# A mixture-of-experts layer on one core: left-over slots of experts 1 to 7 move to the first block, with 32-column float32 matmuls on four column groups for their output

## The chip, the core and the metric

The kernel runs on one core of a Trainium2 chip. A core has five engines that run their own queues of instructions: TensorE (PE; its weight loads are listed apart as PEld), VectorE (DVE), ScalarE (ACT), GpSimd (POOL) and SyncE (SP), which only issues transfers here. They meet through semaphores. The metric is the device time of one execution in microseconds; the time of a kernel is the median of its runs.

## The reference

Local attention (8 heads, chunks of 64) gives 4608 tokens of 512 numbers. A noisy gate picks two of eight experts for each token, and the output is the weighted sum of the two experts' results. This is the part that the change touches:

```python
N, D, E, F = (4608, 512, 8, 1024)
for e in range(E):
    for k in range(2):
        mask = top2[:, k] == e
        h = np.maximum(x[mask] @ w1[e], 0.0)
        out[mask] += top2_w[mask, k, None] * (h @ w2[e])
```

All is in float32, and the result must agree with it to float32 accuracy.

## The kernel before

**Stages.** First attention and the gate, with lists built on the way: for each expert a list of token rows in slots of 128 (`lid`, `lfl`) and of weights (`lwt`). Expert 0 takes its slots first; experts 1 to 7 are ordered by their count on the chip. How many slots a place has is fixed ahead of time (`CAPS`, L30): 1216, 1216, 1184, 1184, 1184, 1152, 1152, 1152. That is nine full tiles of 128 slots for each, and for the first five a left-over tile of 64, 64, 32, 32 and 32. The order of work is written out by hand in the code; each engine runs its instructions in the order of the code.

**Blocks.** `blocks_of` (L37) makes three blocks of each expert: tiles 0 to 2, 3 to 5 and 6 to 9. The left-over tile is the fourth of the third block. Blocks are numbered `i` from 0 to 23, three to an expert. The loop at L698 emits layer 1 of block `i` and then layer 2 of block `i - 1` (blocks 0 to 2 differ a little).

**Layer 1** (`layer1`, L286) computes h transposed: for each of 8 slices `f` of the hidden dimension, 4 x 3 matmuls with a 128x128 piece of W1 as weights and the block's slots as moving columns. Float32 is split into a high and a low part (`xh`, `xl`, `w1h`, `w1l`), and `three` (L277) issues three products of parts in float32r, which are all on L284. ScalarE's Relu writes `hh`, VectorE writes the rest `hl`.

**Layer 2** (`layer2`, L307) turns the roles round: for each tile of up to 128 slots, and each of 8 slices, three matmuls with `hh` or `hl` of the tile as weights and 512 columns of `w2h` or `w2l` moving. A left-over tile of 32 or 64 slots takes the same 24 matmuls of 512 columns as a full one. `weigh` (L301) multiplies by the slots' weights, and `store` (L249) adds the rows to the output in memory by an indirect transfer on POOL.

**Weights.** `w_load` (L109, SP's queue) brings W1 and W2 in four pieces each through four `st` buffers; `w_split` (L119) makes the high and low parts on ScalarE and VectorE. The loads of W1 for expert e + 1 are issued at the block with b = 1 (L700), into the buffers that W2 of expert e leaves when it is split in the same block's layer 1. The split of W1 for e + 1 stands in layer 2 of that block, after layer 1 of the third one.

**Tokens.** From block 3 on, a tile's token rows are fetched in quarters of 32 slots (`gather_some`, L227): an indirect transfer on POOL brings, for 32 slots, 4 pieces of 128 numbers each to 128 partitions, by the indices in `piece`. VectorE turns them in 32x32 squares (`x_tile`, L258). `pieces` (L197) makes these indices in layer 2 of block 1, by four matmuls that spread 32 slots over four groups of partitions; and after it the tiles of block 3 are fetched at once (`gathered(3, 3)`, L734).

Of the kernel before, what the change touches and what calls it, by code (L numbers as in the profile page):

```python
# [8 lines left out]
FT = mybir.dt.float32  # L9
FR = mybir.dt.float32r  # L10
# [3 lines left out]
AF = mybir.ActivationFunctionType  # L14
OP = mybir.AluOpType
# [4 lines left out]
P = 128  # L20
NTOK = 4608
NT = NTOK // P
DM = 512
NE = 8
FF = 1024
ND = DM // P
NF = FF // P
# [9 lines left out]
def blocks_of(cap):  # L37

    rows = [min(P, cap - s) for s in range(0, cap, P)]
    out, cur = [], []  # L40
    for j, r in enumerate(rows):
        cur.append((j, r))
        if len(cur) == 3 and len(rows) - j - 1 != 1:
            out.append(cur)
            cur = []
    if cur:
        out.append(cur)
    return out


@with_exitstack
def kernel(ctx, tc, qT, kT, vh, wgn, noise, w1, w2, out, caps=CAPS):
    nc = tc.nc
    consts = ctx.enter_context(tc.tile_pool(name="consts", bufs=1))
# [35 lines left out]
    for c in sorted(set(caps[1:])):  # L90
        n = caps.index(c, 1)
# [13 lines left out]
    staged = {}  # L105
# [23 lines left out]
    PS = ctx.enter_context(tc.tile_pool(name="psum", bufs=1, space=PSUM)).tile([P, 8, 512], FT, name="PS")  # L129
# [2 lines left out]

    blocks = [blocks_of(c) for c in caps]
    nb = len(blocks[0])
    assert all(len(b) == nb for b in blocks)
    BL = [(e, b) for e in range(NE) for b in range(nb)]
# [1 line left out]
    NJ = NLIST  # L140
    BN = max(sum(r for _, r in b) for bs in blocks for b in bs)
# [15 lines left out]
    lwt = consts.tile([P, NJ, NE], FT, name="lwt")  # L157
    lfl = consts.tile([P, NJ, NE], FT, name="lfl")
    lid0 = {b: consts.tile([P, len(blocks[0][b])], I32, name=f"lid0{b}") for b in EARLY}
    lwt0 = {b: consts.tile([P, len(blocks[0][b])], FT, name=f"lwt0{b}") for b in EARLY}  # L160
    piece = consts.tile([P, 4, NJ, NE], I32, name="piece")
    part = consts.tile([P, 1], FT, name="part")
    nc.vector.memset(part, 0.0)
    for q in range(1, 4):
        nc.vector.memset(part[q * 32:q * 32 + 32], float(q))
    xpieces = xbuf.rearrange("r (q c) -> (r q) c", c=P)
    XG, XH, HT, BX, BH, OB = {}, {}, {}, {}, {}, {}
    rot = {"xg": 0, "tr": 0, "l1": 0, "l2": 0}
    BANKS = {"tr": (0, 1), "l1": (2, 3, 4), "l2": (5, 6)}
# [2 lines left out]
    def bank(what, among=None):  # L172
        among = among or (BANKS if rot["l2"] < 6 else WIDE)[what]
        rot[what] += 1
        return PS[:, among[rot[what] % len(among)], :]

    def rows_of(i, j):
        e = BL[i][0]
        k = j - blocks[0][i][0][0] if i in EARLY else 0
        return lid0[i][:, k:k + 1] if i in EARLY else lid[:, j, e:e + 1]  # L180
# [16 lines left out]
    def pieces():  # L197

        spread = xv[0].tile([P, 4, 4, 32], FT, name="xv")
        nc.vector.tensor_copy(spread, ident.rearrange("p (t c) -> p t c", t=4)[:, :, None, :].to_broadcast([P, 4, 4, 32]))  # L200
        tf = lfl
        for t in range(4):
            p = PS[:, 7, t * NJ * NE:(t + 1) * NJ * NE]
            nc.tensor.matmul(p, spread[:, t].rearrange("p a c -> p (a c)"), tf.rearrange("p j e -> p (j e)"),
                             start=True, stop=True)
        nc.vector.tensor_scalar(piece.rearrange("p t j e -> p (t j e)"), PS[:, 7, 0:4 * NJ * NE],
                                4.0, part, op0=OP.mult, op1=OP.add)

# [37 lines left out]

    stores = {}

    def store(i, e, j, r, o):  # L249
        nc.gpsimd.memset(spacer, 0.0)  # L250
        s = nc.gpsimd.indirect_dma_start(  # L251
            out=out, out_offset=bass.IndirectOffsetOnAxis(ap=rows_of(i, j)[0:r], axis=0),
            in_=o[0:r], in_offset=None, compute_op=OP.add)
        for o in stores.setdefault(e, []):
            tc.declare_no_dep(s.ins, o.ins, reason="an expert has a token once; rows below 128 get zeros and are not read")
        stores[e].append(s)
# [29 lines left out]
    def layer1(i, hook, hook_d=lambda f, d: None):  # L286
        e, b = BL[i]
        n = sum(r for _, r in blocks[e][b])
        HT[i] = BH[i % 2]
        for f in range(NF):  # L290
            p = bank("l1", (0, 1) if i == 0 else None)[:, 0:n]
            for d in range(ND):
                three(p, W[e, 1, d], (slice(None), slice(f * P, (f + 1) * P)),
                      XH[i], (slice(None), d, slice(0, n)), d == 0, d == ND - 1)
                hook_d(f, d)
            hh, hl = HT[i][f]
            nc.scalar.activation(hh[:, 0:n], p, AF.Relu)  # L297
            nc.vector.scalar_tensor_tensor(hl[:, 0:n], p, 0.0, hh[:, 0:n].bitcast(FT), op0=OP.max, op1=OP.subtract)  # L298
            hook(f)

    def weigh(i, j, r, p):  # L301
        e = BL[i][0]
        o = OB[0].tile([P, DM], FT, name="o")
        nc.vector.tensor_scalar(o[0:r], p[0:r], weights_of(i, j)[0:r], None, op0=OP.mult)  # L304
        store(i, e, j, r, o)

    def layer2(i, hook):  # L307
        e, b = BL[i]
        tiles = blocks[e][b]
        for k, (j, r) in enumerate(tiles):  # L310
            p = bank("l2")
            for f in range(NF):
                three(p[0:r], W[e, 2, f // 2], (slice(None), slice((f % 2) * DM, (f % 2) * DM + DM)),
                      HT[i][f], (slice(None), slice(k * P, k * P + r)), f == 0, f == NF - 1, flip=True)
                hook(k, f)
            weigh(i, j, r, p)
            if i > 1:
                gather_some(2)
# [354 lines left out]
    pb = ExitStack()  # L673

    def block_bufs(q):
        pool = pb.enter_context(tc.tile_pool(name=f"blk{q}", bufs=1))
        BX[q] = tuple(pool.tile([P, ND, BN], FR, name=f"x{c}{q}") for c in "hl")
        BH[q] = [tuple(pool.tile([P, BN], FR, name=f"h{c}{q}{f}") for c in "hl") for f in range(NF)]

    block_bufs(0)  # L680
    attend(NT)
# [16 lines left out]
    for i in range(NBL + 1):  # L698
        e, b = BL[i] if i < NBL else (NE, 0)
        if b == 1 % nb and e + 1 < NE and i > 1:  # L700
            for c in range(4):
                w_load(e + 1, 1, c)
        split2 = halves if i < NBL and (b == 1 % nb if e else b == 0) else []
        nxt = blocks[BL[i + 1][0]][BL[i + 1][1]] if i + 1 < NBL else []

        def turn_next(k):
            gathered(i + 1, k)
            x_tile(i + 1, k)
            ahead[0] -= 1

        def hook1(f):
            if i > 1 and b != 1 and f % 2 == 1 and f // 2 < len(nxt):
                turn_next(f // 2)
            if split2:
                w_split(e, 2, *split2[f])
            if i > 1:
                gather_some(1 + f % 2, HT[i][f][0])

        def hook2_f(k, f):
            if i > 1 and b == 1 and f % 4 == 1 and 2 * k + f // 4 < len(nxt):  # L720
                turn_next(2 * k + f // 4)
            if (k, f) == (0, 3):
                for q in split1:
                    w_split(split1_e, 1, *q)

        def hook2_r(k, f):
            hook2_f(k, f)
            step_route(2)
            if k + 1 < len(nxt) or i == 0:
                if f == 6 and k < len(nxt):  # L730
                    x_tile(i + 1, k)
            if i == 1 and (k, f) == (0, 0):
                pieces()
                gathered(3, 3)  # L734

        if 1 < i < NBL and i == 3:
            layer2(i - 1, hook2_f)
        if i < NBL:
            layer1(i, hook1, hook_tail if i == 0 else lambda f, d: None)
        split1 = halves if (i < NBL and b == nb - 1 and e + 1 < NE) else []  # L740
        split1_e = e + 1

        if i == 0:
            pa.close()
            block_bufs(1)
            OB[0] = pb.enter_context(tc.tile_pool(name="ob", bufs=4))
        if i == 0:
            zero_out(NT)
            layer2(0, hook2_r)
            finish_route()  # L750
            for r in range(1, NE):
                place[r] = nc.values_load(order[0:1, r:r + 1], engines=[mybir.EngineType.SP], min_val=0, max_val=NE - 1)
            for c in range(4):
                w_load(1, 1, c)
            pg.close()
            later_xg.append(pb.enter_context(tc.tile_pool(name="xg2", bufs=3)))
            xy = pb.enter_context(tc.tile_pool(name="xy", bufs=2))
            xv.append(pb.enter_context(tc.tile_pool(name="xv", bufs=1)))
        elif i == 1:
            layer2(1, hook2_r)  # L760
            x_tile(2, 3)
        elif i != 2 and i != 3:
            layer2(i - 1, hook2_f)
        if split1:
            for c in range(4):
                w_load(e + 1, 2, c)
# [132 lines left out]
```

## Time and profile before

| what | value |
|---|---|
| median of 3 runs | 1031.76 us (1029.02 to 1033.64) |
| profiled execution | 1033.37 us, its span 1031.5 us |
| mean granted TensorE clock | 0.981 |
| matmuls of L284, layer 1 (3 products) | 3 x 768, mean 340 to 342 ns |
| matmuls of L284, layer 2 (3 products) | 3 x 616, mean 390 to 391 ns |
| gathers on POOL (L239) | 257, mean 1022 ns |
| stores on POOL (L251) | 77, mean 1587 ns |

A profile's span runs from the first to the last instruction; the execution's own time is somewhat longer. Records of matmuls overlap, because TensorE starts one before the last one has drained: a mean of 390 ns is the length of a record, and the distance between starts is what a matmul takes of the path. A shape such as `128*32 128x512` is rows times columns of the weights, then partitions times elements that move.

### The profile page before, as it was taken

What the parts mean: (1) busy time and instruction counts of PE and PEld (TensorE: products, weight loads), DVE (VectorE), ACT (ScalarE), POOL (GpSimd) and SP (SyncE); (2) the same over time, 40 slices, a digit from 0 to 9 for tenths busy, and PEclk for the clock granted to TensorE, in tenths of its full rate; (3) what the DMA queues carried; (4) which work ended last, traced back from release to release, by engine and by line L of the source; (5) the groups of instructions that cost most, each with busy time, mean ns of one, the idle gap of its engine ahead of it and who ended that gap; (6) DMA issues with size and microseconds to landing.
All of it is one profiled execution on the core that took longest, in us unless ns stands there. A gap on an engine that the chain in (4) does not pass through costs nothing.

```text
span 1031.5 us, 17805 instructions
## 1 busy us (share of the span) xinstructions
PE 978.0 (95%) x7121; PEld 866.5 (84%) x7121; DVE 462.0 (45%) x1030; ACT 298.3 (29%) x617; POOL 479.6 (46%) x612
## 2 busy tenths in 40 slices
PE   6778978989999999999999999999999999999995
PEld 5666757887889889888988998899889998999884
DVE  5686665562525443344334432453245334533311
ACT  3565554331314221222222321232123222322100
POOL 1142422445675666157714772378428724801111
PEclk9989888999999999999999999999999999999998
DMA  9987891142442452345224423443334334412213
GB/s 370 402 326 256 280 388 51 41 113 67 95 105 82 95 133 57 58 101 138 54 53 104 130 60 49 103 136 61 51 111 122 77 54 106 135 19 31 31 21 42
DMA packets 51445, 121.48 MB, mean 118 GB/s; under 512 B 8272, under 2 KB 8528, under 8 KB 51360
## 3 DMA queue, kind: packets, MB, share of 16 engines
q0 software_dynamic: 19664, 38.69, 21.7%
q1 hardware_dynamic: 26512, 72.20, 19.3%
q10 hardware_dynamic: 5184, 9.44, 2.4%
q8 instruction: 56, 0.92, 0.4%
q14 instruction: 29, 0.24, 0.1%
HBM read 81.56 MB, written 38.73 MB: 117 GB/s over the span
## 4 chain that ended last, share of the span: by engine, by line
PE 89%; DVE 5%; DMA 2%; ACT 1%; issue 1%; POOL 0%; SPq 0%; ACTq 0%; DVEq 0%; POOLq 0%
PE PS L284 80%; PE PS L397 2%; PE PS L549 2%; PE PS L370 2%; DMA out<-zero 1%; PE PS L386 1%; PE PS L417 1%; DVE xs L409 1%; DVE mx L374 1%; DVE pr L379 1%; PE PS L435 1%; DMA xbuf<-xs 1%; PE PS L424 1%; DMA kb<-in_kT 0%; PE PS L267 0%
## 5 line engine op out<-in xcount | busy, mean ns | idle before, releaser
L239 POOL DMA_INDIRECT xg<-xbuf,piece x257 | 262.7, 1022 | 75.9 <-issue 70.4
L251 POOL DMA_INDIRECT out<-o,lid x77 | 122.2, 1587 | 316.7 <-DVE o L304 301.4
L284 PE MATMUL PS<-xh,w1h 128*128 128x384 f32 (+2 forms) x768 | 262.5, 342 | 1.9 <-DVE xl L275 1.4
L284 PE MATMUL PS<-xl,w1h 128*128 128x384 f32 (+2 forms) x768 | 260.8, 340 | 0.4 <-DVE xl L275 0.4
L284 PE MATMUL PS<-xh,w1l 128*128 128x384 f32 (+2 forms) x768 | 260.8, 340 | 0.0
L284 PE MATMUL PS<-w2h,hh 128*128 128x512 f32 x616 | 240.6, 391 | 0.0
L284 PE MATMUL PS<-w2h,hl 128*128 128x512 f32 x616 | 240.2, 390 | 0.0
L284 PE MATMUL PS<-w2l,hh 128*128 128x512 f32 x616 | 240.2, 390 | 0.0
L297 ACT ACTIVATE hh<-PS 128x384 fp32r<-128x384 f32 (+2 forms) x192 | 95.2, 496 | 474.5 <-PE PS L284 474.5
L298 DVE SCALAR_TENSOR_TENSOR hl<-PS,hh 128x384 fp32r<-128x384 f32 (+2 forms) x192 | 108.6, 566 | 193.0 <-ACT hh L297 193.0
L304 DVE TENSOR_SCALAR o<-PS,lwt 128x512 f32<-128x512 f32 x77 | 57.6, 749 | 242.6 <-PE PS L284 242.6
L284 PEld LDWEIGHTS PS<-xh,w1h 128*128 128x128 f32 x768 | 144.5, 188 | 5.4 <-DVE xl L275 1.7
L284 PEld LDWEIGHTS PS<-xl,w1h 128*128 128x128 f32 x768 | 144.6, 188 | 2.4 <-DVE xl L275 0.7
L284 PEld LDWEIGHTS PS<-xh,w1l 128*128 128x128 f32 x768 | 144.6, 188 | 0.9
L284 PEld LDWEIGHTS PS<-w2h,hl 128*128 128x128 f32 x616 | 112.9, 183 | 27.1
L284 PEld LDWEIGHTS PS<-w2l,hh 128*128 128x128 f32 x616 | 112.9, 183 | 26.1
L284 PEld LDWEIGHTS PS<-w2h,hh 128*128 128x128 f32 x616 | 112.9, 183 | 25.8
L274 ACT ACTIVATE xh<-y 128x512 fp32r<-128x512 f32 x67 | 41.2, 614 | 93.2 <-DVE y L271 93.2
L275 DVE TENSOR_TENSOR xl<-y,xh 128x512 fp32r<-128x512 f32 x67 | 45.1, 673 | 48.3 <-ACT xh L274 48.3
L557 POOL TENSOR_SCALAR gohp<-row_p,gpf 128x128 f32<-128x128 f32 x36 | 24.6, 715 | 66.4 <-DVE gpf L541 53.5
L397 PE MATMUL PS<-vb,pts 64*64 64x65 f32 x1152 | 29.4, 242 | 17.5 <-DVE xs L409 11.3
L271 DVE STREAM_TRANSPOSE y<-xg 128x512 f32<-128x512 f32 x67 | 45.6, 681 | 0.0
(130 smaller groups left out, 770.8 us busy)
## 6 DMA issues: line engine op xcount, KB each, us to landing
st<-in_w SPq DMA_DIRECT2D x64, 512.0 KB, 5.1
out<-zero SPq DMA_DIRECT2D x37, 256.0 KB, 4.6
vb<-in_vh SPq DMA_DIRECT2D x18, 520.0 KB, 3.9
qp<-in_qT SPq DMA_DIRECT2D x18, 512.0 KB, 7.2
kb<-in_kT SPq DMA_DIRECT2D x18, 512.0 KB, 9.0
xbuf<-xs ACTq DMA_DIRECT2D x36, 256.0 KB, 6.1
xg<-xbuf,piece POOLq DMA_INDIRECT x257, 2.6
out<-o,lid POOLq DMA_INDIRECT x77, 4.9
```

The costliest lines, as they stand in the source:

```text
L239: nc.gpsimd.indirect_dma_start(out=XG[e, j][:, t * P:(t + 1) * P], out_offset=None, in_=xpieces, in_offset=bass.IndirectOffsetOnAxis(ap=pi ...
L251: s = nc.gpsimd.indirect_dma_start(out=out, out_offset=bass.IndirectOffsetOnAxis(ap=rows_of(i, j)[0:r], axis=0), in_=o[0:r], in_offset=Non ...
L271: nc.vector.transpose(y[:, 0:4 * r], x[:, 0:4 * r])
L274: nc.scalar.activation(oh, src, AF.Copy)
L275: nc.vector.tensor_sub(ol, src, oh.bitcast(FT))
L284: nc.tensor.matmul(p, a, b, start=first and n == 0, stop=last and n == 2)
L297: nc.scalar.activation(hh[:, 0:n], p, AF.Relu)
L298: nc.vector.scalar_tensor_tensor(hl[:, 0:n], p, 0.0, hh[:, 0:n].bitcast(FT), op0=OP.max, op1=OP.subtract)
L304: nc.vector.tensor_scalar(o[0:r], p[0:r], weights_of(i, j)[0:r], None, op0=OP.mult)
L370: nc.tensor.matmul(PS[s, h, o:o + 64], q[r, t % 2, hp, s], k[r, t % 2, hp, s], start=True, stop=True)
L397: nc.tensor.matmul(PS[s, 3 + h, hp * 65:hp * 65 + 65], PT[t][r, hp, s], v[r, t % 2, c, hp, :], start=True, stop=True)
L557: nc.gpsimd.tensor_scalar(ohp[:, 0], row_p, pf[:, 0, 0, r:r + 1], None, op0=OP.is_equal)
```

## The change

`blocks_tail` replaces `blocks_of` for experts 1 to 7: the left-over tile is now the fourth of the first block, tiles 6 to 8 are the third. In layer 1 the left-over slots' part of h gets a Relu of its own, into a new float32 tile `hf`, and no high and low part. In layer 2 of the first block, `tail2` computes these slots' output ahead of the full tiles: for 32 slots at a time, and each slice `f`, four float32 matmuls with the same 32 columns of `hf` as weights; each has 128 of the 512 columns of raw W2 (the `st` buffer) moving, and writes to 32 partitions of its own. So the 32 slots' 512 numbers come out as four pieces on 128 partitions, like the gathered tokens. The weights are spread over the partitions in the same way (`wrep`, four more matmuls in `pieces`), and the store goes by `piece`, 128 pieces of 128 numbers. Expert 0 is as before.

```diff
+def blocks_tail(cap):
+
+    full = [(j, P) for j in range(cap // P)]
+    out = [full[n:n + 3] for n in range(0, len(full), 3)]
+    if cap % P:
+        out[0] = out[0] + [(cap // P, cap % P)]
     return out
...
-    blocks = [blocks_of(c) for c in caps]
+    blocks = [blocks_of(caps[0])] + [blocks_tail(c) for c in caps[1:]]
...
+    wrep = consts.tile([P, 4, NE], FT, name="wrep")
...
+    opieces = out.rearrange("r (q c) -> (r q) c", c=P)
+    HF = {}
...
+            nc.tensor.matmul(PS[:, 7, 4 * NJ * NE + t * NE:4 * NJ * NE + (t + 1) * NE],
+                             spread[:, t].rearrange("p a c -> p (a c)"), lwt[:, NJ - 1, :], start=True, stop=True)
+        nc.vector.tensor_copy(wrep.rearrange("p t e -> p (t e)"), PS[:, 7, 4 * NJ * NE:4 * (NJ + 1) * NE])
...
-    def store(i, e, j, r, o):
+    def store(e, to, rows, o):
         nc.gpsimd.memset(spacer, 0.0)
         s = nc.gpsimd.indirect_dma_start(
-            out=out, out_offset=bass.IndirectOffsetOnAxis(ap=rows_of(i, j)[0:r], axis=0),
-            in_=o[0:r], in_offset=None, compute_op=OP.add)
+            out=to, out_offset=bass.IndirectOffsetOnAxis(ap=rows, axis=0),
+            in_=o, in_offset=None, compute_op=OP.add)
...
-            nc.scalar.activation(hh[:, 0:n], p, AF.Relu)
-            nc.vector.scalar_tensor_tensor(hl[:, 0:n], p, 0.0, hh[:, 0:n].bitcast(FT), op0=OP.max, op1=OP.subtract)
+            r = blocks[e][b][-1][1] % P if e else 0
+            m = n - r
+            if r:
+                nc.scalar.activation(HF[0][:, f, 0:r], p[:, m:n], AF.Relu)
+                p = p[:, 0:m]
+            nc.scalar.activation(hh[:, 0:m], p, AF.Relu)
+            nc.vector.scalar_tensor_tensor(hl[:, 0:m], p, 0.0, hh[:, 0:m].bitcast(FT), op0=OP.max, op1=OP.subtract)
             hook(f)
+
+    def tail2(e, j, r):
+
+        for t in range(r // 32):
+            p = bank("l2")
+            for f in range(NF):
+                w = staged[e, 2, f // 2][:, (f % 2) * DM:(f % 2) * DM + DM]
+                for q in range(4):
+                    nc.tensor.matmul(p[32 * q:32 * q + 32, 0:P], HF[0][:, f, 32 * t:32 * t + 32], w[:, q * P:(q + 1) * P],
+                                     start=(f == 0), stop=(f == NF - 1))
+            o = OB[0].tile([P, DM], FT, name="o")
+            nc.vector.tensor_scalar(o[:, 0:P], p[:, 0:P], wrep[:, t, e:e + 1], None, op0=OP.mult)
+            store(e, opieces, piece[:, t, j, e:e + 1], o[:, 0:P])
...
-        store(i, e, j, r, o)
+        store(e, out, rows_of(i, j)[0:r], o[0:r])
...
     def layer2(i, hook):
         e, b = BL[i]
         tiles = blocks[e][b]
+        if e and tiles[-1][1] < P:
+            tail2(e, *tiles[-1])
+            tiles = tiles[:-1]
...
-        BH[q] = [tuple(pool.tile([P, BN], FR, name=f"h{c}{q}{f}") for c in "hl") for f in range(NF)]
+        BH[q] = [tuple(pool.tile([P, HN], FR, name=f"h{c}{q}{f}") for c in "hl") for f in range(NF)]
...
+            HF[0] = pb.enter_context(tc.tile_pool(name="hf", bufs=1)).tile([P, NF, max(c % P for c in caps[1:])], FT, name="hf")
```

Three places show what this does to the order of instructions. The first is TensorE at the end of block 5's layer 2 before the change (the third block of expert 1): the start of the left-over tile's 24 matmuls, with the numbered parts of W2 and of h.

```order
L284 MATMUL PS<-w2h_4223,hh_3124 64x512
L284 MATMUL PS<-w2l_4224,hh_3124 64x512
L284 MATMUL PS<-w2h_4223,hl_3125 64x512
L284 MATMUL PS<-w2h_4223,hh_3126 64x512
L284 MATMUL PS<-w2l_4224,hh_3126 64x512
L284 MATMUL PS<-w2h_4223,hl_3127 64x512
```

After the change these and the 18 that follow are gone, and the 32-slot tiles of experts 2 to 4 likewise. The second place is TensorE in the changed kernel where layer 1 of block 4 ends and layer 2 of block 3 begins (the first block of expert 1).

```order
L299 MATMUL PS<-xh_2620,w1h_3954 128x384
L299 MATMUL PS<-xl_2621,w1h_3954 128x384
L299 MATMUL PS<-xh_2620,w1l_3955 128x384
L328 MATMUL PS<-st,hf 32x128 x64
L299 MATMUL PS<-w2h_4247,hh_3125 128x512
L299 MATMUL PS<-w2l_4248,hh_3125 128x512
```

The 64 on L328 are new, two sets of 8 x 4 for the 64 slots of expert 1; experts 2 to 4 have 32 each at the same place. The rows around them stood next to each other before. The third place is SP's queue, at the four loads of W1 for expert 2 and the first of W2 behind them; before:

```order
L113 DMA st<-in_w 128x1x1024 [waits DMAHW6_49,DVE_49]
L113 ISA
L113 DMA st<-in_w 128x1x1024 [waits DMAHW7_49,DVE_49]
L113 ISA
L113 DMA st<-in_w 128x1x1024 [waits DMAHW0_49,DVE_49]
L113 ISA
L113 DMA st<-in_w 128x1x1024 [waits DMAHW1_49,DVE_49]
L115 ISA
L115 DMA st<-in_w 128x2x512 [waits DMAHW2_49,DVE_49]
```

And in the changed kernel:

```order
L122 DMA st<-in_w 128x1x1024 [waits DMAHW6_49,DVE_49,PE_49]
L122 ISA
L122 DMA st<-in_w 128x1x1024 [waits DMAHW7_49,DVE_49,PE_49]
L122 ISA
L122 DMA st<-in_w 128x1x1024 [waits DMAHW0_49,DVE_49,PE_49]
L122 ISA
L122 DMA st<-in_w 128x1x1024 [waits DMAHW1_49,DVE_49,PE_49]
L124 ISA
L124 DMA st<-in_w 128x2x512 [waits DMAHW2_49,DVE_49]
```

The four loads stand where they did, but wait for TensorE too: for the matmuls on L328, which read the raw W2 that lies in the buffers. The loads of W2 behind them wait for what they waited for before.

More of the change, by code (lines that the diff above doesn't have):

```diff
@@ L47, in blocks_of @@
         out.append(cur)
+    return out
+def blocks_tail(cap):
[3 more added lines that the diff above has]
+        out[0] = out[0] + [(cap // P, cap % P)]
     return out
@@ L676, in block_bufs @@
         pool = pb.enter_context(tc.tile_pool(name=f"blk{q}", bufs=1))
+        HN = BN if q == 0 else 3 * P
         BX[q] = tuple(pool.tile([P, ND, BN], FR, name=f"x{c}{q}") for c in "hl")
-        BH[q] = [tuple(pool.tile([P, BN], FR, name=f"h{c}{q}{f}") for c in "hl") for f in range(NF)]
+        BH[q] = [tuple(pool.tile([P, HN], FR, name=f"h{c}{q}{f}") for c in "hl") for f in range(NF)]
     block_bufs(0)
```

## The prediction

> **What bounds the kernel now.** I read the page first: the busy shares, the slices, and the chain of work that ended last.
>
> ```profile
> PE 978.0 (95%) x7121; PEld 866.5 (84%) x7121; DVE 462.0 (45%) x1030; ACT 298.3 (29%) x617; POOL 479.6 (46%) x612
> ...
> PE   6778978989999999999999999999999999999995
> ...
> PE 89%; DVE 5%; DMA 2%; ACT 1%; issue 1%; POOL 0%; SPq 0%; ACTq 0%; DVEq 0%; POOLq 0%
> PE PS L284 80%; PE PS L397 2%; PE PS L549 2%; PE PS L370 2%; DMA out<-zero 1%; PE PS L386 1%; PE PS L417 1%; DVE xs L409 1%; DVE mx L374 1%; DVE pr L379 1%; PE PS L435 1%; DMA xbuf<-xs 1%; PE PS L424 1%; DMA kb<-in_kT 0%; PE PS L267 0%
> ```
>
> The chain is TensorE for 89%, and four fifths of the span are one line, the split matmuls of both layers (L284). A share is only an average, so next I read the busy times by stretch, cut where the experts' work starts. The columns are the stretch, its length, then busy time and count of PE, PEld, DVE, ACT and POOL, the granted clock, and the DMA's share.
>
> ```profile
> 235.00:297.00 62.00, 60.25 (x286) 49.82 (x285) 21.46 (x35) 12.61 (x24) 42.24 (x50) 1.00 0.43 95
> 297.00:527.00 230.00, 230.00 (x1154) 206.25 (x1153) 94.45 (x154) 57.14 (x111) 136.49 (x180) 1.00 0.38 86
> 527.00:772.00 245.00, 245.00 (x1227) 219.06 (x1225) 101.46 (x165) 61.43 (x119) 127.42 (x159) 1.00 0.38 87
> 772.00:1019.60 247.60, 247.60 (x1249) 224.57 (x1247) 91.65 (x148) 54.23 (x106) 100.35 (x124) 1.00 0.33 66
> ```
>
> From 297 us to the last matmul TensorE is busy the whole time at a granted clock of 1.00, and the busiest other engine, POOL, is at 59% (136.49 of 230) or below. The view of TensorE's waits for 297 to 1019 us is empty, while that for 190 to 297 us has four small entries (in each: what waits, for what, total us, times, longest):
>
> ```profile
> PE PS L549 <- DVE geq L561: 3.4, 1, 3.4
> PE PS L204 <- DVE xv L200: 0.9, 1, 0.9
> PE PS L284 <- ACT xh L274: 0.5, 1, 0.5
> PE PS L284 <- DVE xl L275: 0.4, 1, 0.4
> ```
>
> So whatever TensorE no longer has to do after 297 us comes off the end, one for one, until another engine becomes late. All the change's main edits lie there.
>
> **What is removed.** The left-over tiles of experts 1 to 4 (64, 32, 32, 32 slots) each took 24 matmuls of 512 columns in layer 2: 8 slices of the hidden dimension, 3 products. The shape groups show how many, and the timeline shows from where to where (start, duration, what):
>
> ```profile
> L284 PE MATMUL PS<-w2h,hh 128*32 128x512 f32 x24 | 9.5, 394 | 0.0
> L284 PE MATMUL PS<-w2h,hh 128*64 128x512 f32 x16 | 6.3, 393 | 0.0
> ...
> 415.93 0.40 PE L284 MATMUL PS<-w2h,hh 128*64 128x512 f32 x1
> ...
> 421.45 0.33 PE L284 MATMUL PS<-xh,w1h 128*128 128x384 f32 x1
> ...
> 521.75 0.39 PE L284 MATMUL PS<-w2h,hh 128*32 128x512 f32 x1
> ...
> 527.31 0.34 PE L284 MATMUL PS<-xh,w1h 128*128 128x384 f32 x1
> ```
>
> The x24 of one product are three 32-slot tiles of 8, the x16 two 64-slot tiles, of which one is expert 0's and stays. A mean of 394 ns is no price, since pipelined records overlap; the start of the tile to the start of what follows is. That is 421.45 - 415.93 = 5.52 us for 64 slots and 527.31 - 521.75 = 5.56 us for 32 (0.23 us a matmul: a tile of 32 rows costs what one of 128 does). Removed: 5.52 + 3 x 5.56 = **22.2 us**.
>
> **What is added on TensorE.** Each 32 slots now take 8 x 4 float32 matmuls of 128 columns, on four column groups; there are 2 + 1 + 1 + 1 = 5 such sets. The trace has no such matmul, but it has its two halves: the gate's (L424), with the same 32-column weights on the same four column groups and 512 columns, and the scores' (L370), four quadrants and 64 columns.
>
> ```profile
> 45.33 0.49 PE L386 MATMUL PS<-ident,pr 128*128 128x128 f32 x3
> 45.66 0.60 PE L417 MATMUL PS<-ident,xs 128*128 128x128 f32 x4
> 46.19 1.06 PE L424 MATMUL PS<-xt,wg 128*32 128x512 f32 x8
> 47.18 0.45 PE L370 MATMUL PS<-kb,qp 64*64 64x64 f32 x14
> ...
> 46.19 0.16 PEld L424 LDWEIGHTS PS<-xt,wg 128*32 128x32 f32 x8 [0.17 <-issue]
> ...
> L424 PE MATMUL PS<-xt,wg x72: 592/605/819, 31.7 to 173.8; 128*32 128x512 f32 x72
> ...
> 49.69 0.96 PE L435 MATMUL PS<-sel,ls 128*128 128x16 f32 x8
> 50.58 0.69 PE L370 MATMUL PS<-kb,qp 64*64 64x64 f32 x32
> ...
> L370 PE MATMUL PS<-kb,qp x1152: 218/218/367, 5.8 to 144.4; 64*64 64x64 f32 x192
> ```
>
> Four float32 matmuls of L424 appear as 8 instructions, so each is two passes; the 8 end 1.06 us after the first began, though each takes 0.605. One after another they could not, so the groups run side by side, in two rounds of four, 1.06 - 0.605 = 0.455 us apart. By columns that is 0.455 / 4 = 0.114 us for 128. L370's 32 instructions are 8 rounds of four: (0.69 - 0.218) / 7 = 0.067 us a round of 64 columns; the line through both points gives 0.123 at 128. I take 0.118 us between the two. Below, a round is bounded by the three single 128-column float32 transposes of L386, (45.66 - 45.33) / 3 = 0.110 us each; above, by twice L370's round, 0.134.
>
> A set is 8 x 4 x 2 / 4 = 16 rounds, five sets 80: 80 x 0.118 = **9.4 us** (8.8 to 10.7). Going into and out of the column groups costs a little: L417's last transpose starts at about 45.66 + 3 x 0.110 = 45.99 and L424 starts 0.09 later than one more transpose would; at its end, 47.18 - 46.19 = 0.99 is 0.08 more than two rounds of 0.455. Eight such changes: **0.7 us**. The lower end is 0; the upper is 1.3, if each time the rest of a running matmul shows, by which a record outlasts the spacing (0.39 - 0.23 = 0.16 us).
>
> The Trainium skill has a rule that speaks against the change here: TensorEngine Tiling (Array Packing), Key Properties, says that a change of the tiling mode drains TensorE. By it the sum would be at that upper end, 0.6 us worse. The trace shows less: the old 32-slot tile took 5.56 us where a third of a layer 2 of full tiles, (347.12 - 330.75) / 3, takes 5.46 (rows below), so its two changes together cost 0.1.
>
> **The pieces stage** (L197) gets four more matmuls of 8 columns, which will be 8 instructions with 128-column weights. L435 has 8 of 16 columns in 0.96 us, so **1.0 us** (0 to 1.0). It is on the path: TensorE is busy 60.25 of 62 us there. The copy into `wrep` stands ahead of the piece indices and can delay the gathers by some tenths of a microsecond; the tiles that these serve are turned only under the next block's layer 1.
>
> **What lies beside other work.** Layer 1 has the same columns, in the first block instead of the third, with 96 matmuls a block before and after: nothing. ScalarE gets 32 short Relus and VectorE loses as much as it gets; both are under 42% busy after 297 us. POOL issues one store more (5 for 4), now of 128 pieces:
>
> ```profile
> L251 POOL DMA_INDIRECT out<-o,lid x77 | 122.2, 1587 | 316.7 <-DVE o L304 301.4
> ...
> 238.72 0.96 POOL L239 DMA_INDIRECT xg<-xbuf,piece  x1 [10.19 <-issue]
> 239.99 0.95 POOL L239 DMA_INDIRECT xg<-xbuf,piece  x1 [0.30 <-issue]
> ...
> 252.49 0.94 POOL L239 DMA_INDIRECT xg<-xbuf,piece  x1 [0.30 <-issue]
> ```
>
> At 1.59 us each and with 301 us of waiting for `o` on that line, nothing. After the pieces 14 gathers instead of 12 stand ahead of the next stores; at 239.99 - 238.72 = 1.27 us that ends at about 257 us, and the last of them serves the fourth tile, which is turned at the end of block 2's layer 1 (it ends at 275.58, next rows). Nothing.
>
> **The added wait.** The raw W2 buffers are now held until the new matmuls have read them, so the next expert's four W1 loads on the SP queue wait for TensorE, where they waited for VectorE's split. Behind them in the queue stand only the W2 loads, which wait for the W1 split anyway.
>
> ```profile
> 275.58 0.39 PE L284 MATMUL PS<-w2h,hh 128*128 128x512 f32 x1
> ...
> 330.75 0.39 PE L284 MATMUL PS<-w2h,hh 128*128 128x512 f32 x1
> ...
> 347.12 0.36 PE L284 MATMUL PS<-xh,w1h 128*128 128x448 f32 x1
> ...
> 320.30 13.01 SPq L113 DMA_DIRECT2D st<-in_w  x4
> 369.26 3.99 SPq L115 DMA_DIRECT2D st<-in_w  x4
> ...
> DMA to landing us min/median/max: 8.0/8.0/8.0
> ...
> 367.27 4.27 ACT L126 ACTIVATE w1h<-st 128x512 fp32r<-128x512 f32 x8
> ```
>
> Before, the four went out from 320.30 to 333.31, and were split from 367.27 on. Now they go out once the set is done, about 4 us after the block's layer 1 ended and layer 2 began (330.75): 335 to 339 at the pace of the four L115 loads, landing by 339 + 8 = 347 us. That is 20 us early. Nothing; what it would cost without that margin is a rival.
>
> **The sum.** -22.2 + 9.4 + 0.7 + 1.0 = **-11.1 us**. The profiled execution took 1033.37 us (span 1031.5), so 1022.3 by its own account. It lies 1.6 us above the median of the three runs, 1031.76; against that the forecast is **1020.6 us**, 1.1% faster.
>
> **Rivals.**
>
> *Weight loads that show.* If each round of 32-column loads stood ahead of its matmuls instead of beside those before, a round would be longer by one load, whose record has a mean of 0.111 us:
>
> ```profile
> L424 PEld LDWEIGHTS PS<-xt,wg 128*32 128x32 f32 x72 | 1.5, 111 | 3.5 <-ACT xt L418 2.0 <-issue 1.5
> ```
>
> 80 x 0.229 = 18.3, and the sum is -22.2 + 18.3 + 0.7 + 1.0 = -2.2: **1029.6 us**, no difference. For it: a set has 64 loads for 64 short matmuls, where L424 has 8 for long ones. Against it: L424's 8 loads are over 0.16 us after the first, while its matmuls run for 1.06, and L370's rounds of 0.067 us are shorter than a load. The Trainium skill has such a rule: TensorE: Matmul & The Clock Gate, Part 3, The mechanism, lets a weight load overlap running matmuls only where the row groups differ, and all four column groups use all rows; L424's second four loads disagree. Chance 6%.
>
> *Column groups that take turns* (the slower side). With four different 128-column slices of W2 to read, the groups might be served one at a time, at L386's 0.110 us for each of 320 instructions: 35.2 us, the sum -22.2 + 35.2 + 0.7 + 1.0 = +14.7: **1046.5 us**. The kernel gets slower as soon as a round takes over (22.2 - 1.7) / 80 = 0.256 us. For it: nothing in the trace runs 128-column slices this way. Against it: L424 reads four different slices too, and they overlap. Chance 4%.
>
> *W1 comes late.* Should the loads take over 28 us instead of 8, TensorE would wait ahead of the first block of experts 2 to 5: each further 5 us there gives +20, 1040.6 us in all. The only landing in the records is 8.0. Chance 3%.
>
> *The gain is hidden.* If another engine took over at once, nothing would move: 1031.8 us. Against it: the empty view of waits and POOL at 59% or less. Chance 4%.
>
> **How the numbers follow.** The forecast's own case keeps 83%. Its bounds are -22.2 + 8.8 = -13.4 at the least and -22.2 + 10.7 + 1.3 + 1.0 = -9.2 at the most: 1018.4 to 1022.6. The three runs lie 2.7 below to 1.9 above their median; with that on each side it is 1015.7 to 1024.5, and I widen the upper side to 1026 for loads that show in part (a third of the first rival). 0.5% (5.2 us) is about what a measurement can tell from no change: the forecast's case lies beyond it throughout. Faster 0.84, with part of the first rival; same 0.10; slower 0.06, the second and third.
>
> **What would show it right or wrong.** Right: the removed shapes (128*64 for expert 1, 128*32 with 512 columns) are gone, `PS<-st,hf` stands four times in the timeline, about 2.0 us from start to start of what follows for 32 slots and 3.9 for 64; the waits of TensorE after 297 us stay empty; the pieces stage has 16 instructions in about 2 us. Wrong: a round over 0.14 us (loads that show, or turns), a wait for `w1h` or `w1l` at the start of a first block, or a busy POOL ahead of `xl`.

## The result and the profile after

| | before | changed |
|---|---|---|
| median of 6 runs, side by side | 1032.7 us (1028.76 to 1034.12) | 1021.17 us (1019.39 to 1022.63) |
| ratio to before | 1 | 0.9892, 95% interval 0.9874 to 0.991 |
| profiled execution, its span | 1033.37, 1031.5 us | 1020.17, 1018.3 us |

The kernel is 1.1% faster: 11.5 us less, where 11.1 were forecast (1020.6 us). The page of the changed kernel, the lines that answer to those of before:

```profile
PE 965.4 (95%) x7353; PEld 863.5 (85%) x7353; DVE 459.7 (45%) x1032; ACT 299.8 (29%) x649; POOL 484.3 (48%) x613
...
PE 88%; DVE 5%; DMA 3%; ACT 1%; issue 1%; SPq 1%; ACTq 0%; DVEq 0%
PE PS L299 79%; DMA out<-zero 2%; PE PS L585 2%; PE PS L406 1%; PE PS L433 1%; PE PS L422 1%; PE PS L453 1%; PE PS L328 1%; DVE pr L415 1%; DVE mx L410 1%; DVE xs L445 1%; PE PS L460 1%; DMA xbuf<-xs 1%; SPq L662 1%; PE PS L471 1%
```

The shares hardly move, though the span is 13 us shorter in these two profiles (3 of the 13 are gained ahead of 190 us, by chance, as the first experiment shows): TensorE bounded the kernel and still does. The shape of the path shows in the stretches (length, then busy time and count of PE, PEld, DVE, ACT, POOL, the clock, DMA), cut where they were cut for the kernel before, the last at its last matmul:

```profile
235.00:297.00 62.00, 61.16 (x289) 50.85 (x289) 22.29 (x37) 12.79 (x24) 43.72 (x54) 1.00 0.42 94
297.00:527.00 230.00, 230.00 (x1322) 210.69 (x1322) 94.78 (x158) 60.70 (x139) 141.23 (x181) 1.00 0.38 86
527.00:772.00 245.00, 245.00 (x1354) 224.16 (x1354) 104.02 (x172) 63.29 (x131) 136.94 (x168) 1.00 0.39 90
772.00:1005.90 233.90, 233.84 (x1170) 210.75 (x1168) 85.13 (x139) 50.21 (x98) 89.48 (x111) 1.00 0.33 66
```

TensorE is still busy throughout, and POOL, the next, is at 61% (141.23 of 230). The view of TensorE's waits from 190 us on has the same four small entries as before, all ahead of 297 us:

```profile
PE PS L585 <- DVE geq L597: 3.4, 1, 3.4
PE PS L216 <- DVE xv L212: 0.9, 1, 0.9
PE PS L299 <- ACT xh L289: 0.5, 1, 0.5
PE PS L299 <- DVE xl L290: 0.4, 1, 0.4
```

So no wait took the place of the removed work. The new sets stand where the order put them. TensorE's timeline around expert 2's set (start, duration, what), from the start of layer 1 of block 7 to that of block 8:

```profile
419.20 0.33 PE L299 MATMUL PS<-xh,w1h 128*128 128x384 f32 x1
...
435.96 1.96 PE L328 MATMUL PS<-st,hf 128*32 128x128 f32 x64
437.85 0.50 PE L299 MATMUL PS<-w2h,hh 128*128 128x512 f32 x1
...
454.32 0.33 PE L299 MATMUL PS<-xh,w1h 128*128 128x384 f32 x1
```

From start to start the 64 instructions take 437.85 - 435.96 = 1.89 us, for which 5.56 were spent before. The stretch of 454.32 - 419.20 = 35.12 us holds one layer 1, one set and three full tiles of layer 2; it is the ruler for the experiments.

The pieces stage is the other place, from the start of layer 2 of block 1 to that of layer 1 of block 2, in the kernel before:

```profile
234.54 0.39 PE L284 MATMUL PS<-w2h,hh 128*128 128x512 f32 x1
...
255.38 0.47 PE L284 MATMUL PS<-xh,w1h 128*128 128x448 f32 x1 [0.47 <-ACT xh L274]
```

and in the changed one:

```profile
231.78 0.39 PE L299 MATMUL PS<-w2h,hh 128*128 128x512 f32 x1
...
253.56 0.47 PE L299 MATMUL PS<-xh,w1h 128*128 128x448 f32 x1 [0.47 <-ACT xh L289]
```

It went from 20.84 to 21.78 us: 0.94 more. (Three more profiles with the same eight instructions have 21.75.)

### The profile page after: what moved, and what is told of

The parts are those of the page before. It is cut to its first block, busy times and chain, and to the rows that moved or that the text cites. A ratio compares the mean times of both kernels' runs of the same rounds, so it can differ in the third digit from the quotient of the medians.

```text
span 1018.3 us, 18328 instructions
## 1 busy us (share of the span) xinstructions
PE 965.4 (95%) x7353; PEld 863.5 (85%) x7353; DVE 459.7 (45%) x1032; ACT 299.8 (29%) x649; POOL 484.3 (48%) x613
## 4 chain that ended last, share of the span: by engine, by line
PE 88%; DVE 5%; DMA 3%; ACT 1%; issue 1%; SPq 1%; ACTq 0%; DVEq 0%
PE PS L299 79%; DMA out<-zero 2%; PE PS L585 2%; PE PS L406 1%; PE PS L433 1%; PE PS L422 1%; PE PS L453 1%; PE PS L328 1%; DVE pr L415 1%; DVE mx L410 1%; DVE xs L445 1%; PE PS L460 1%; DMA xbuf<-xs 1%; SPq L662 1%; PE PS L471 1%
## 5 line engine op out<-in xcount | busy, mean ns | idle before, releaser
L254 POOL DMA_INDIRECT xg<-xbuf,piece x257 | 266.2, 1036 | 77.2 <-issue 60.0
L266 POOL DMA_INDIRECT out<-o,lid x73 | 116.7, 1599 | 243.5 <-DVE o L337 227.0
L299 PE MATMUL PS<-w2h,hh 128*128 128x512 f32 x584 | 228.5, 391 | 0.0
L299 PE MATMUL PS<-w2h,hl 128*128 128x512 f32 x584 | 227.6, 390 | 0.0
L299 PE MATMUL PS<-w2l,hh 128*128 128x512 f32 x584 | 227.6, 390 | 0.0
L317 ACT ACTIVATE hh<-PS 128x384 fp32r<-128x384 f32 (+1 forms) x192 | 94.1, 490 | 371.3 <-PE PS L299 371.3
L318 DVE SCALAR_TENSOR_TENSOR hl<-PS,hh 128x384 fp32r<-128x384 f32 (+1 forms) x192 | 107.2, 559 | 193.4 <-ACT hh L317 193.4
L299 PEld LDWEIGHTS PS<-w2h,hl 128*128 128x128 f32 x584 | 109.2, 187 | 23.5
L299 PEld LDWEIGHTS PS<-w2h,hh 128*128 128x128 f32 x584 | 109.2, 187 | 23.1 <-issue 0.8
L299 PEld LDWEIGHTS PS<-w2l,hh 128*128 128x128 f32 x584 | 109.2, 187 | 22.5
```

The costliest lines, as they stand in the source:

```text
L254: nc.gpsimd.indirect_dma_start(out=XG[e, j][:, t * P:(t + 1) * P], out_offset=None, in_=xpieces, in_offset=bass.IndirectOffsetOnAxis(ap=pi ...
L266: s = nc.gpsimd.indirect_dma_start(out=to, out_offset=bass.IndirectOffsetOnAxis(ap=rows, axis=0), in_=o, in_offset=None, compute_op=OP.add)
L299: nc.tensor.matmul(p, a, b, start=first and n == 0, stop=last and n == 2)
L317: nc.scalar.activation(hh[:, 0:m], p, AF.Relu)
L318: nc.vector.scalar_tensor_tensor(hl[:, 0:m], p, 0.0, hh[:, 0:m].bitcast(FT), op0=OP.max, op1=OP.subtract)
```

## The experiments

The theory: after 297 us the time is TensorE's own program. A left-over tile's 24 matmuls go (22.2 us for the four); five sets of 16 rounds come, side by side on four column groups; going there and back costs something; the move of the tiles itself is worth nothing. The rivals are named at each experiment.

The first four experiments ran on another chip, where the kernel before was some 9 us later too (median 1041.3 us); the four profiles taken there show one wait of 7.4 to 7.5 us ahead of block 2's layer 1 (last section). So times are compared as ratios to before on the same chip, and stretches only after 297 us.

### The move alone

Layer 1 makes high and low parts of all slots again, `layer2` treats the left-over tile as its fourth, and `pieces` is as before:

```diff
-            r = blocks[e][b][-1][1] % P if e else 0
+            r = 0
...
-        if e and tiles[-1][1] < P:
-            tail2(e, *tiles[-1])
-            tiles = tiles[:-1]
```

> The left-over tiles stand in the first block as in the change, but their output is made as before, by 24 split matmuls of 512 columns, and the pieces stage is as before. If the whole gain is the shorter layer 2 of these tiles (the sum of the prediction), four tiles cost 5.5 us each again, 22.2 us in all, nothing else moves, and the time is that of the kernel before within 0.3% (1030 to 1036 where before is 1032.7). If moving the tiles to the first block brings a part by itself (a better place for the turning of tokens, another layout of buffers), this kernel is 3 us or more faster than before. The 3 us by which the changed kernel's profile is ahead before 190 us: if they belong to the move, layer 2 of block 0 starts near 187 us here too; if they are chance, anywhere from 186 to 191.

Measured: 1042.78 us, ratio 1.0013 (0.9997 to 1.003). Its timeline has the tile of expert 2 at its new place:

```profile
466.32 0.39 PE L295 MATMUL PS<-w2h,hh 128*32 128x512 f32 x1
...
471.88 0.34 PE L295 MATMUL PS<-xh,w1h 128*128 128x384 f32 x1
```

5.56 us, as before. The move brings nothing that the times can tell: the gain is in how the output is made. Layer 2 of block 0 starts at 190.50 us here; in the ten profiles of this study it starts between 186.08 and 191.93, and in the changed kernel's second profile at 188.24. The 3 us by which its first one was ahead there, at 187.10 against 190.11, lie within what the executions differ by.

### No output for the left-over slots

This leaves out layer 2 of the left-over slots of experts 1 to 7.

```diff
-            tail2(e, *tiles[-1])
```

> Leaves out layer 2 of the left-over slots of experts 1 to 4; all else is the changed kernel. If TensorE's own program is the path, the time falls by just what the sets take in the changed kernel's timeline: 3.63 + 3 x 1.88 us, and 4 x 0.21 us by which the matmuls around them are longer, 10.1 us in all: about 1011 us. If another engine stands close behind TensorE, less than 5 us are gained and TensorE shows waits after 297 us.

Measured: 1020.05 us where before is 1041.32, ratio 0.9799 (0.9775 to 0.9823); the changed kernel has 0.9892. The 0.93% between them are 9.6 us of 1032.7, beside the 10.1 read from the timeline. The same stretch as above:

```profile
423.52 0.33 PE L299 MATMUL PS<-xh,w1h 128*128 128x384 f32 x1
...
456.55 0.33 PE L299 MATMUL PS<-xh,w1h 128*128 128x384 f32 x1
```

33.03 us, so a set with all that it brings costs expert 2 35.12 - 33.03 = 2.09 us, of which 0.2 are not in its own 1.89. TensorE shows no wait after 297 us here either, so no other engine stands close behind it in the 10 us beyond the change.

### The same matmuls on one column group

```diff
-                    nc.tensor.matmul(p[32 * q:32 * q + 32, 0:P], HF[0][:, f, 32 * t:32 * t + 32], w[:, q * P:(q + 1) * P],
+                    nc.tensor.matmul(p[32 * t:32 * t + 32, q * P:(q + 1) * P], HF[0][:, f, 32 * t:32 * t + 32], w[:, q * P:(q + 1) * P],
```

The loop over `q` goes outside the one over `f`, and the store is by rows.

> The same 320 float32 matmul instructions of 128 columns, but each set on one column group: the four slices of W2 go to four ranges of columns of the same 32 partitions, and the store is by rows again. If four groups side by side are what pays, a set takes 64 x 0.110 = 7.0 us in place of 1.75, 35.2 in all, and the kernel is 26 us slower than the changed one: about 1047 us, 15 slower than before. If float32 in place of three split products pays whatever the groups (raw W2, no splitting of h), it stays within 5 us of the changed kernel.

Measured: 1056.02 us, ratio 1.0135 (1.011 to 1.016): slower than before. Its 320 instructions are the same in number and shape as the changed kernel's; the shape groups of the changed kernel and then of this one:

```profile
L328 PE MATMUL PS<-st,hf 128*32 128x128 f32 x320 | 9.6, 274 | 0.0
```

```profile
L328 PE MATMUL PS<-st,hf 128*32 128x128 f32 x320 | 35.3, 273 | 0.0
```

Each record lasts the same 0.27 us, but the time that they cover together is 9.6 against 35.3 us. A mean of records says nothing of a price; what makes this change pay is that the groups run side by side. Float32 in place of the split products, on one group, loses 14 us.

### Two visits in place of one

```diff
-            for f in range(NF):
+            for f in fs:
...
+            if rest and k == 0:
+                tail2(e, *rest, range(NF // 2, NF), ps)
```

> Each set is cut in two: slices 0 to 3 ahead of the first full tile of layer 2, slices 4 to 7 behind it. The matmuls are the same, but TensorE goes into and out of the column groups eight times more. If such a change costs 0.17 us (1.37 us for eight, which the changed kernel's timeline leaves once 80 rounds of 0.109 us are taken off), the stretch of layer 1's end to layer 2's end is 0.34 us longer for each of experts 1 to 4, 1.4 us in all. If it costs 0.085 us, as the prediction had it, 0.7 us; if the rounds themselves are longer and the change is nearly free, under 0.3 us.

Measured (a single run, 1032.23 us where before is 1041.32), the stretch for expert 2:

```profile
430.33 0.33 PE L299 MATMUL PS<-xh,w1h 128*128 128x384 f32 x1
...
447.10 1.08 PE L329 MATMUL PS<-st,hf 128*32 128x128 f32 x32
448.11 0.50 PE L299 MATMUL PS<-w2h,hh 128*128 128x512 f32 x1
...
453.79 1.08 PE L329 MATMUL PS<-st,hf 128*32 128x128 f32 x32
454.80 0.50 PE L299 MATMUL PS<-w2h,hh 128*128 128x512 f32 x1
...
465.81 0.33 PE L299 MATMUL PS<-xh,w1h 128*128 128x384 f32 x1
```

35.48 us against 35.12: one more visit costs 0.36 us, 0.18 a change. The stretches of experts 3 and 4 grow by the same 0.36, so four more visits cost the expected 1.4. Half of a set takes 1.01 us from start to start, more than half of 1.89; that is 0.13 of the 0.36. Most of the rest lies in the matmuls on both sides. The second half starts 0.31 us after the full tile's last matmul (453.48), where matmuls of that shape are otherwise 0.23 apart, and the first record after a set is 0.50 us long, where others of its shape have 0.39.

### Half as many columns

This leaves out half of the left-over slots' output of experts 1 to 7: `w[:, q * P:q * P + P // 2]` moves in place of all 128 columns.

> Leaves out half of the left-over slots' output of experts 1 to 7: each of the 320 instructions moves 64 columns in place of 128. A round of four took 0.109 us in the changed kernel, and a weight load's record is 0.110 us long, so the two can't be told apart there. If the moving columns set the round and the loads are hidden, a round falls to 0.055 to 0.067 us and a 32-slot set to about 1.0 to 1.2 us. If the loads set it, a round stays at 0.11 and the set at 1.9 us.

Measured (a single run, 1017.97 us where before is 1032.51):

```profile
419.72 0.33 PE L299 MATMUL PS<-xh,w1h 128*128 128x384 f32 x1
...
436.48 1.10 PE L328 MATMUL PS<-st,hf 128*32 128x64 f32 x64
437.51 0.50 PE L299 MATMUL PS<-w2h,hh 128*128 128x512 f32 x1
...
453.98 0.33 PE L299 MATMUL PS<-xh,w1h 128*128 128x384 f32 x1
```

34.26 us, 0.86 less than with 128 columns: 64 columns fewer make each of the 16 rounds 0.054 us shorter. The length of a round can be read with expert 1, whose 64 slots have 16 rounds more than expert 2's set and no further visit. Its rows here:

```profile
334.05 1.99 PE L328 MATMUL PS<-st,hf 128*32 128x64 f32 x128
335.98 0.50 PE L299 MATMUL PS<-w2h,hh 128*128 128x512 f32 x1
```

From start to start expert 1's set takes 1.93 us and expert 2's 1.03, so a round is 0.90 / 16 = 0.056 us. In the changed kernel the two take 3.63 (its rows stand with the reasons why the prediction was right) and 1.89, so a round of 128 columns is 1.74 / 16 = 0.109 us. Without the rounds, 2.09 - 1.74 = 0.35 us are left there and 1.23 - 0.90 = 0.33 here, where 1.23 is 34.26 - 33.03: the visit, by a second way about the 0.36 of above. The weight loads do not set the pace. In the changed kernel they look as if they might:

```profile
L328 PEld LDWEIGHTS PS<-st,hf 128*32 128x32 f32 x320 | 8.5, 110 | 1.0 <-issue 1.0
```

A record of 110 ns beside a round of 109 is a coincidence: with half the columns the loads are as long (shortest, median and longest in ns), and yet the rounds take 56 ns.

```profile
L328 PEld LDWEIGHTS PS<-st,hf x320: 106/110/110, 334.0 to 640.4; 128*32 128x32 f32 x160
```

The Trainium skill (TensorE: Matmul & The Clock Gate, Part 3, The mechanism) says that a load overlaps running matmuls only where the row groups differ; the same section also lets a load into a background weight buffer go ahead of them. The first statement alone does not hold for these column groups, which all use the same rows, nor for the kernel before, where from 297 to 527 us the loads were busy for 206.25 of 230 us beside matmuls, nearly all on the whole array, that were busy for all 230. Whether a background buffer is what makes it possible, no run shows.

### Float32 without column groups

Eight float32 matmuls of 512 columns with 128 columns of weights, on the whole array; what they compute for the left-over slots is not the reference's.

```diff
-                for q in range(4):
-                    nc.tensor.matmul(p[32 * q:32 * q + 32, 0:P], HF[0][:, f, 32 * t:32 * t + 32], w[:, q * P:(q + 1) * P],
+            nc.tensor.matmul(p, HF[0][:, g:g + 2, :].rearrange("p a c -> p (a c)"), w, start=(f == 0), stop=(f == NF - 1))
```

> Each left-over tile's output is made by 8 float32 matmuls of 512 columns with 128 columns of weights on the whole array (the weights hold other slots' values too, and for slice 7 those of slice 6: what is computed for the left-over slots is not the reference's). This goes from split products to float32 and back at the same places, without column groups. If it is the column groups that cost 0.34 us a visit, the matmuls around are as without a visit: layer 1 ahead 16.67 us, layer 2 behind 16.36, and 16 instructions take 16 x 0.427 to 16 x 0.455 us. If it is the change to float32 and back, layer 1 ahead stays at 16.76 and layer 2 behind at 16.48, as in the changed kernel.

Measured (a single run, 1040.87 us where before is 1032.51):

```profile
426.41 0.33 PE L299 MATMUL PS<-xh,w1h 128*128 128x384 f32 x1
...
443.07 0.59 PE L327 MATMUL PS<-st,hf 128*128 128x512 f32 x1
...
449.54 0.79 PE L299 MATMUL PS<-w2h,hh 128*128 128x512 f32 x1
...
466.30 0.33 PE L299 MATMUL PS<-xh,w1h 128*128 128x384 f32 x1
```

Read by the parts that were expected, it fits neither: layer 1 ahead takes 443.07 - 426.41 = 16.66 us (no cost of going in), layer 2 behind 466.30 - 449.54 = 16.76 (0.40 more), and the 16 instructions 6.47, less than 16 x 0.427 = 6.83. The first record of layer 2 starts early and lasts 0.79 us, so the border between the two is not a real one; that step of the expectation was badly chosen. The whole stretch is: 39.89 - 33.03 = 6.86 us. From the second of the 16 instructions (443.50) to the last (449.51) they start 0.429 us apart, and 16 x 0.429 = 6.86: nothing is left for going to float32 and back. So the 0.36 us come with the 32-column weights in float32, not with float32 alone.

Nor do they need the four groups side by side. The kernel of the run on one column group keeps expert 2's set on the first 32 columns of the array, and its stretch is:

```profile
440.96 0.33 PE L299 MATMUL PS<-xh,w1h 128*128 128x384 f32 x1
...
457.72 7.17 PE L328 MATMUL PS<-st,hf 128*32 128x128 f32 x64
464.82 0.50 PE L299 MATMUL PS<-w2h,hh 128*128 128x512 f32 x1
...
481.30 0.33 PE L299 MATMUL PS<-xh,w1h 128*128 128x384 f32 x1
```

That is 40.34 us, 7.31 above the kernel without output. Its 64 instructions, 0.109 us apart, are 7.0 of them, and 0.3 are left, about a visit again: one group alone pays it.

### A leaner pieces stage, and the changed kernel again

In the first, `lfl` and the weights of the left-over slots stand in one tile, and four matmuls of 88 columns do for the eight of 80 and 8:

```diff
-            nc.tensor.matmul(p, spread[:, t].rearrange("p a c -> p (a c)"), tf.rearrange("p j e -> p (j e)"),
+            nc.tensor.matmul(p, spread[:, t].rearrange("p a c -> p (a c)"), lfw.rearrange("p j e -> p (j e)"),
                              start=True, stop=True)
-            nc.tensor.matmul(PS[:, 7, 4 * NJ * NE + t * NE:4 * NJ * NE + (t + 1) * NE],
-                             spread[:, t].rearrange("p a c -> p (a c)"), lwt[:, NJ - 1, :], start=True, stop=True)
```

> The weights of the left-over slots go into the same four matmuls as the rows (88 columns in place of 80 and 8 apart), so 8 instructions go from the pieces stage. By the sum the stage's 0.93 us come back and the rest stays: 0.8 to 0.9 us less between the start of layer 2 of block 1 and of layer 1 of block 2, and a time 0.1% below the changed kernel's, which a time can't tell. If the pieces stage is bound by VectorE or ScalarE rather than TensorE, the stretch stays as it is.

> The changed kernel once more, beside the others on this chip: 0.9874 to 0.991 of before. Its early stages, up to layer 2 of block 0, show whether the 3 us by which its first profile was ahead there come again (near 187 us) or are chance (186 to 191).

Measured, side by side: 1022.11 us, ratio 0.9894 (0.9873 to 0.9915), and 1022.8 us, 0.991 (0.989 to 0.993). The stage in the leaner kernel:

```profile
236.35 0.39 PE L299 MATMUL PS<-w2h,hh 128*128 128x512 f32 x1
...
257.27 0.47 PE L299 MATMUL PS<-xh,w1h 128*128 128x448 f32 x1 [0.47 <-ACT xh L289]
```

20.92 us: 0.86 of the 0.94 are back, so TensorE was the bound there. The intervals of the two kernels overlap; that this one's stage is shorter is read from the trace, not from the times.

Expert 2's stretch in all the kernels, on one ruler (the changed kernel's second profile has 35.12 again):

| kernel | stretch, us | above no output | what it is |
|---|---|---|---|
| no output | 33.03 | | layer 1 and three full tiles |
| half the columns | 34.26 | 1.23 | 16 rounds of 0.056, one visit |
| changed | 35.12 | 2.09 | 16 rounds of 0.109, one visit |
| two visits | 35.48 | 2.45 | 16 rounds of 0.109, two visits |
| the move alone | 38.59 | 5.56 | 24 split matmuls of 0.232 |
| float32, whole array | 39.89 | 6.86 | 16 instructions of 0.429 |
| one column group | 40.34 | 7.31 | 64 instructions of 0.109, one visit |

## Why the prediction was right

The time came out 0.6 us from the forecast. The gain is the sounder comparison, because before itself has 1032.7 us beside the changed kernel and not the 1031.76 that the forecast started from: 11.5 us (9.3 to 13.0 by the interval) for 11.1. The parts came out as follows.

- **Removed, 22.2 us**: right. With the move alone the tile stands there with its 5.56 us, and the ratio is 1.
- **80 rounds at 0.118, 9.4 us**: the rounds run side by side as predicted, but one takes 0.109 us, 8.7 us in all. The estimate lay between two rows that both take in the first round after a change of grouping, and that round is longer. L424's second round starts 0.45 us after its first, where float32 instructions of 512 columns on the whole array are 0.43 apart; L370's second round starts 0.11 us after its first, the next one 0.06 later. So part of a visit was in the price of a round. The lower bound, the transposes' spacing of 0.110 us, was the better row.
- **Eight changes of grouping, 0.7 us**: too small by half. They cost 4 x 0.36 = 1.4 us, just above the upper end of 1.3. Two steps failed. The first is the reading of L424's neighbours, 0.09 us going in and 0.08 coming out. In the changed kernel's timeline of expert 2's set, going in costs 0.10 (the set starts 0.27 after the matmul ahead of it, where 0.17 is usual), the first round 0.02, the last round 0.11, and the first matmul behind the set 0.10 (the next one starts 0.33 after it, where 0.23 is usual). L424 could not show that last part, because no whole-array matmul stands behind it. The second is the step by which the old 32-slot tile, at 0.1 us for going in and out, spoke against the drain. Its starts in the kernel before are 0.23 us apart at both ends and within; the 0.1 us is spread over its 24 matmuls and is no price of a change. So split products with 32 columns of weights pay nothing at the ends, float32 alone pays nothing, and float32 with 32 columns of weights pays 0.36. The Trainium skill (TensorEngine Tiling (Array Packing), Key Properties) has it that a change of mode drains TensorE. That fits this price, and the upper end that the prediction drew from it was nearly right; whether the 0.36 us is a drain, and why the old tile was spared, no run shows.
- **The two errors cancel**: predicted 10.1 us for the sets and changes; read from the timelines, 335.46 - 331.83 = 3.63 and the 0.2 beside it for expert 1 (next rows), and 2.09 for each of three, 10.1 again. Rounds 0.7 us too dear in all and changes 0.7 us too cheap cancel, and that they do so to 0.1 us is luck. The total was better than its terms.
- **Pieces, 1.0 us**: 0.94, of which 0.86 went away again with the eight instructions.
- **What was costed at nothing**: right as far as the trace can say. The ratio of the move alone is 1, and TensorE's list of waits is unchanged; POOL's five new stores and the short Relus show in neither.
- **The added wait**: the loads of W1 for expert 2 went out from 334.28 to 340.34 us (forecast 335 to 339), and their split starts at 370.41. The one landing recorded took 7.6 us. The margin of 20 us is there, so this rival never came into play.

Expert 1's set in the changed kernel's timeline of TensorE:

```profile
331.83 3.70 PE L328 MATMUL PS<-st,hf 128*32 128x128 f32 x128
335.46 0.50 PE L299 MATMUL PS<-w2h,hh 128*128 128x512 f32 x1
```

The loads of W1 on SP's queue, and ScalarE's split of them, each from its own timeline of the same kernel:

```profile
334.28 6.06 SPq L122 DMA_DIRECT2D st<-in_w  x4
```

```profile
370.41 4.26 ACT L135 ACTIVATE w1h<-st 128x512 fp32r<-128x512 f32 x8
```

- **The rivals**: weight loads that show are ruled out by the rounds of 0.056 us. Groups that take turns would have given 1046.5 us; forced onto one group the matmuls give 1.0135 of before, which is 1046.6 at its 1032.7. The price of that rival was right, but the changed kernel's groups do not take turns. The hidden gain is ruled out by the gain itself, and the kernel without output gains 9.6 of the expected 10.1 us more.

## What to carry to other kernels

Where one engine's program is the path and its waits are empty, price an edit by the distance between starts at the place it stands, never by the length of records: the same 320 records of 0.27 us were worth 9.6 or 35.3 us. Here a matmul with few columns of weights cost as much as a full one (5.56 against 5.46 us a tile), and became cheap only when others stood beside it on the other column groups; then count the rounds, and add what a visit costs, here about 0.35 us, so that what goes to the groups is better done in one piece. When a forecast comes out right, check its terms: two here were off by 0.7 us each, in opposite directions.

## What was not expected of the hardware

On the chip of the first four experiments, TensorE waits once for 7.5 us ahead of block 2's layer 1. In the profile of the kernel without output, ScalarE starts to copy two turned tiles only 6.5 us after TensorE had turned the second (252.06), and the profile names no engine of the core as what released it, only "remote". The timeline of all engines (the turns, the copies, and the first matmul that needs them, with the idle time ahead of each):

```profile
250.36 0.60 PE L282 MATMUL PS<-ident,xg 128*128 128x128 f32 x4
...
251.59 0.47 PE L282 MATMUL PS<-ident,xg 64*128 64x64 f32 x4
...
258.60 0.87 ACT L289 ACTIVATE xh<-PS 128x512 fp32r<-128x512 f32 x2 [12.18 <-remote]
...
259.52 0.74 PE L299 MATMUL PS<-xh,w1h 128*128 128x448 f32 x1 [7.47 <-ACT xh L289]
```

In the six other profiles the same wait is 0.5 us. What held ScalarE up was not found. It came in all four kernels profiled on that chip, each with 12.2 us of idle ScalarE put down to "remote". The kernel before was not profiled there, but its times are as late as theirs, so the ratios stand.
